# First batch's first half: pair 2's division moved behind row copies, pair 3's product moved to VectorE, the first gate groups issued a step sooner

## The chip, the cores and the metric

The kernel runs on one core of one Trainium2 chip. The metric is the device time of one execution in microseconds. The core's engines work side by side and wait for one another through semaphores: TensorE (PE in the profile; its weight loads are PEld), VectorE (DVE), ScalarE (ACT), GpSimd (POOL) and SyncE (SP), which here only issues DMAs. Each engine takes its instructions in the order in which the program lists them for it.

## The reference

Inputs are `q`, `k`, `v` of shape (4, 8, 768, 64) (batch, head, token, width), 16 centroids per head, and three weight matrices. The first stage is attention inside clusters, the second a gated feed-forward layer on its output:

```python
q_assign = np.argmax(np.einsum('bhsd,hcd->bhsc', q_n, c_n), axis=-1)
k_assign = np.argmax(np.einsum('bhsd,hcd->bhsc', k_n, c_n), axis=-1)
mask = q_assign[:, :, :, None] == k_assign[:, :, None, :]
scores = scale * np.matmul(q, k.transpose(0, 1, 3, 2))
scores = np.where(mask, scores, -1000000000.0)
...
attn = attn / (np.sum(attn, axis=-1, keepdims=True) + 1e-09)
return np.matmul(attn, v).astype(np.float32)
...
gate = 1.0 / (1.0 + np.exp(-(x @ w_gate)))
val = x @ w_val
return (gate * val @ w_out).astype(np.float32)
```

`x` holds the 3072 tokens by 512 (8 heads of 64); `w_gate` and `w_val` are 512 x 1536, `w_out` is 1536 x 512.

## The kernel before

Heads are worked in four pairs per batch. For each head the kernel splits `q` and `k` into a high and a low 16-bit part (`hl`), turns them so that the width lies across partitions (`T`), multiplies with the centroids (`lg`, logits), takes the largest (`mx`) and writes a one-hot row per token (`oh`). The one-hots are turned too (`oh_ps`) and copied into rows 64 to 79 of `T`: these are the **row copies** (L1396 for the keys, L1400 for the queries of a part, on DVE or, at L1398, on ACT). So one matmul `sc` (L1066) gives score and mask at once. ACT takes the exponential `es` (L1071), and three short matmuls `av` (L1089) multiply it with the values, to which a column is added that sums the weights.

A **step** is one such piece: 128 keys of a head against 384 queries, one `sc`, one `es`, three `av`. There are 384 steps. The `av` of a step stand a few steps behind its `sc` (three in the first batch, `la0`). The first batch is cut into two halves of its queries: all eight heads on the first 384 tokens (steps 0 to 47), then all eight on the others.

When both heads of a pair are through, `normalise2` (first batch; later batches use `normalise`) ends them: DVE adds a correction `sv` to the sums `av` and writes `t` (L384), DVE takes the reciprocal `rec` of the weight column (L389), POOL multiplies and writes `xp` (L390). In the first half, and for pair 0 of the second, `turn_x` then turns `xp` on PE (`x_ps`, L1117) and DVE copies the result into `xTb` (L1118), which the feed-forward layer reads.

The feed-forward work is a queue of pieces: for each of 12 column blocks a gate group (four matmuls `g`, L532, and a tanh `th` on ACT, L538), a value group (four matmuls `v`, L548, and a product `hT` on DVE, L553), then output groups (`o`). `ffn_block` puts a half's pieces into the queue at a step that the table sets: the end of its steps plus a lag, `lag00` for the first batch's first half. From then on `ffn_run` takes pieces from the queue at each step, as many as a budget of nanoseconds per step allows (`ns02` is 490).

All other work stands in a table by step too: `SCHED` maps names to steps, counted from the step at which a pair is first used, and `at(step, f)` runs `f` when the loop comes to that step. The order in which the loop writes instructions is the order of each engine. `xt30` and `xm30` set the step of the turn of pair 3's `xp`. `b1p2l20` chooses how the logits of batch 1, pair 2, head 0 are made: not zero takes `logits2`, two matmuls of 16 columns for each of 12 blocks, summed in PSUM (L423); zero takes `logits`, one matmul of 32 columns per block (L436), whose two halves a reduction on DVE then adds (`lgs`, L451). `b1p2lg0` and `b1p2pk0`, -35.5 steps from use, set when this happens. Hops of later heads (DMAs of one-hot rows into `T`) are issued 12 steps or more ahead of use.

Four PSUM banks (`bank`) go round among `sc`, `g`, `v`, `lg` and `x_ps`.

Of the kernel before, what the change touches and what calls it, by code (L numbers as in the profile page):

```python
# [11 lines left out]
ALU = mybir.AluOpType  # L12
# [83 lines left out]
    "fwv": [354, 356, 357, 359, 364, 366, 370, 371], "b3p2pk1": -28.5, "END": 0,  # L96
}


# [1 line left out]
def kernel(  # L101
# [12 lines left out]
    PE, ACT, DVE, POOL, SP = nc.tensor, nc.scalar, nc.vector, nc.gpsimd, nc.sync  # L114
# [250 lines left out]
    def bcast(ap, n):  # L365
        return ap.unsqueeze(len(ap.shape)).to_broadcast(list(ap.shape) + [n])

    def normalise(av, nq, b, p, e, x, eng=None):

        t = tmpp.tile([128, NCH, 65], FP, name="t")  # L370
        sv = SV[b, p][:, e, :].unsqueeze(1).to_broadcast([128, nq, 65])
        DVE.tensor_tensor(t[:, 0:nq, :], av, sv, ALU.add)  # L372
        rec = smp.tile([128, NCH], FP, name="rec")
        DVE.reciprocal(  # L374
            rec[:, 0:nq], t[:, 0:nq, 64:65].rearrange("p c x -> p (c x)")
        )
        (eng or POOL).tensor_tensor(x, t[:, 0:nq, 0:64], bcast(rec[:, 0:nq], 64), ALU.mult)  # L377

    def normalise2(av, nq, b, p, x):
        t = tmpp.tile([128, NCH, 65], FP, name="t")
        sv = SV[b, p].unsqueeze(2).to_broadcast([128, 2, nq, 65])
        DVE.tensor_tensor(  # L384
            t.rearrange("p (e c) d -> p e c d", e=2), av.rearrange("p (e c) d -> p e c d", e=2),
            sv, ALU.add,
        )
        rec = smp.tile([128, NCH], FP, name="rec")
        DVE.reciprocal(rec, t[:, :, 64:65].rearrange("p c x -> p (c x)"))  # L389
        POOL.tensor_tensor(  # L390
            x.rearrange("p c (e d) -> p e c d", e=2),
            t[:, :, 0:64].rearrange("p (e c) d -> p e c d", e=2),
            bcast(rec.rearrange("p (e c) -> p e c", e=2), 64), ALU.mult,
        )

    T = {}

# [676 lines left out]
    def do_av(s):  # L1074
        b, p, e, nq = s["b"], s["p"], s["e"], s["nq"]
        first, last = s.get("first", False), s.get("last", False)
        need(("v", b, p, e))
        both = nq == 3 and b < SCHED.get("pn", 0)
        if first:
            if not both:  # L1080
                cur["av"] = avp.tile([128, nq, 65], FP, tag="av", name="av")
            elif e == 0:
                cur["av"] = avp.tile([128, 2 * nq, 65], FP, tag="av", name="av")
            if e == 0:
                cur["x"] = xpp.tile([128, nq, 128], HP, tag="xp", name="xp")
        av, x = cur["av"], cur["x"]
        a0 = nq * e if both else 0
        for i in range(s["n"]):
            PE.matmul(  # L1089
                out=av[:, a0 + s["c0"] + i, :], lhsT=s["es"][:, bass.ts(i, 128)],  # L1090
                rhs=VA[b, p][:, e, s["j"], :],
                start=(first and i == 0 and a0 == 0),
                stop=(last and i == s["n"] - 1 and (e == 1 or not both)), skip_group_check=True,
            )
        if last:
            if not both:
                normalise(av, nq, b, p, e, x[:, :, bass.ts(e, 64)])
            elif e == 1:
                normalise2(av, nq, b, p, x)
            if e == 1:  # L1100
                f = lambda: turn_x(b, p, x, 128 * s["h0"], nq, s["xT"])
                if b == 0 and SCHED.get(f"xm{p}{3 * s['h1']}", p == 3):
                    at(step_no[0] + SCHED.get(f"xt{p}{3 * s['h1']}", 5), f)
                else:
                    d_ = SCHED.get(f"xs{min(b, 1)}{p}", 0)
                    if d_ > 0 and (b < B - 1 or p < 2):
                        at(step_no[0] + d_, f)
                    else:
                        f()

    def turn_x(b, p, x, o, nq, xT):
        done.update(("x", b, p, o // 128 + c) for c in range(nq))
        dst = xT[:, p, o : o + 128 * nq].rearrange("p (c t) -> p c t", t=128)
        if b == 0 and SCHED.get(f"xm{p}{3 * [z for z, _ in PARTS].index(o // 128)}", p == 3):
            ps = (turns if SCHED.get("lgop", 1) else bank)(NCH * 128, HP, name="x_ps")
            for c in range(nq):
                PE.transpose(ps[:, bass.ts(c, 128)], x[:, c, :], identh)  # L1117
            DVE.tensor_copy(xT[:, p, o : o + 128 * nq], ps[:, 0 : 128 * nq])  # L1118
        else:
            SP.dma_start_transpose(out=dst, in_=x.rearrange("p c t -> p (c t)"))  # L1120

    bg = {}
    step_no = [-4]

    def at(i, f):
        bg.setdefault(max(i, step_no[0] - 0.5), []).append(f)
# [11 lines left out]
    def need(*names):  # L1138
        for n in names:
            assert n in done, n  # L1140
# [441 lines left out]
    for b, p, e in P:  # L1582
        if b + p + e == 0:
            continue
        d = P[b, p, e]
        for k_, o_ in (OFF if b else FIRST).items():
            f = d.get(k_[:2])
# [114 lines left out]
    for b in range(B):  # L1702
# [17 lines left out]
        for p, e, c in heads(b):  # L1720
            for s in head_steps(b, p, e, c):
                s["xT"] = xT
                do_scores(s)
                run_bg(step_no[0] - 0.5)
                pend.append(s)
                r = step_no[0] - BASE[b]
                ns = SCHED.get(f"ns{b}{r // 24}", SCHED.get(f"ns{b}", 500.0))
                ns += SCHED.get(f"nx{step_no[0]}", 0)
                ffn_run(ns if b or r >= DONE0[0] else 0.0)
                while len(pend) > LA[min(b, 1)]:  # L1730
                    do_av(pend.pop(0))
                run_bg(step_no[0])
                step_no[0] += 1
    while pend:
        ffn_run(500.0)
        do_av(pend.pop(0))
# [34 lines left out]
```

## Time and profile before

| | us |
|---|---|
| median of 3 runs | 319.01 |
| lowest and highest | 318.76, 319.01 |
| the profiled execution | 319.12 |
| its span | 317.3 |
| PE busy in the span | 310.0 |
| ACT busy | 244.9 |
| DVE busy | 238.6 |
| POOL busy | 120.9 |

The span runs from the first to the last instruction, and times in rows of the trace count from its start; 1.8 us of the execution lie around it. A row of the timeline gives start, duration, engine, line, operation, output and inputs, shapes and count, and in brackets how long the engine was idle before and what ended that. Matmuls are pipelined: a matmul of 384 columns shows 0.33 us, while the next can start 0.16 us after it.

### The profile page before, as it was taken

Reading aid. Unit: us, or ns where it says so; the run is one execution under the profiler, and the core shown is the slowest. Engines: PE = TensorE matmul, PEld = TensorE weight load, DVE = VectorE, ACT = ScalarE, POOL = GpSimd, SP = SyncE. Lnnn points to the kernel's source line nnn. Section 1 sums busy time; section 2 is a strip of 40 time slices with the busy share of each in tenths; the row PEclk is TensorE's granted clock in tenths of the full one; section 3 lists DMA queues with packets and bytes.
Section 4 is the critical chain, followed back from the end, with each engine's and each line's share of the span. In section 5 each row is a group of like instructions: output and inputs, shape, how many; then the busy total and the mean of one; then the engine's idle time right before and its main releaser. Section 6 shows DMA issues by size and latency. Waiting matters only on the chain.

```text
span 317.3 us, 9228 instructions
## 1 busy us (share of the span) xinstructions
PE 310.0 (98%) x3492; PEld 218.8 (69%) x3492; DVE 238.6 (75%) x623; ACT 244.9 (77%) x555; POOL 120.9 (38%) x157
## 2 busy tenths in 40 slices
PE   7899999999999999999999999999999999999995
PEld 4688766766666666666777678766677678656685
DVE  5899756778688777686788688776888776678983
ACT  6688998797899887877776876777877887588621
POOL 5888454244434275423234333424212111026600
PEclk9999999999999999999999999999999999999999
DMA  7999998639848988976676455882506130300014
GB/s 196 379 259 169 271 164 143 176 83 264 242 100 163 204 221 136 199 217 161 106 193 153 151 118 134 248 153 53 112 2 76 55 27 14 145 1 3 0 35 165
DMA packets 77996, 45.16 MB, mean 142 GB/s; under 512 B 56896, under 2 KB 75520, under 8 KB 77952
## 3 DMA queue, kind: packets, MB, share of 16 engines
q1 hardware_dynamic: 73840, 39.66, 51.3%
q0 software_dynamic: 3680, 4.72, 9.1%
q8 instruction: 27, 0.44, 0.6%
q10 hardware_dynamic: 432, 0.20, 0.2%
q14 instruction: 17, 0.14, 0.1%
HBM read 28.34 MB, written 6.29 MB: 109 GB/s over the span
## 4 chain that ended last, share of the span: by engine, by line
PE 93%; DMA 2%; DVE 1%; POOL 1%; SPq 1%; issue 0%; ACT 0%; DVEq 0%
PE sc L1066 19%; PE g L532 15%; PE v L548 15%; PE av L1089 11%; PE o L994 9%; PE o L865 5%; PE lg L436 2%; PE o L699 2%; PE o_end L802 2%; PE av L699 2%; DMA kraw<-in_k_dram 2%; PE v L628 2%; PE y L699 2%; PE o L802 1%; PE av L802 1%; PE z L699 1%
## 5 line engine op out<-in xcount | busy, mean ns | idle before, releaser
L1071 ACT ACTIVATE es<-sc 128x384 f16<-128x384 f32 x384 | 174.1, 492 | 38.5 <-PE sc L1066 29.8
L1066 PE MATMUL sc<-T 128*128 128x384 f16 x384 | 117.3, 325 | 0.7 <-DVE T L1396 0.4
L1089 PEld LDWEIGHTS <-es 128*128 128x128 f16 x1152 | 81.3, 98 | 35.1 <-ACT es L1071 0.2
L1089 PE MATMUL av<-va,es 128*128 128x65 f16 x1152 | 97.6, 194 | 0.0
L553 DVE SCALAR_TENSOR_TENSOR hT<-th,v 128x384 f16<-128x384 f32 x72 | 39.8, 553 | 33.8 <-PE av L1089 29.6
L377 POOL TENSOR_TENSOR xp<-t,rec 128x384 f16<-128x384 f32 (+1 forms) x30 | 21.8, 726 | 97.3 <-DVE rec L374 49.2
L548 PE MATMUL v<-xTb,wv 128*128 128x384 f16 x288 | 58.5, 326 | 0.1
L532 PE MATMUL g<-xTb,wg 128*128 128x384 f16 x288 | 58.5, 326 | 0.0
L538 ACT ACTIVATE th<-g 128x384 f32<-128x384 f32 x72 | 35.4, 492 | 8.3 <-PE g L532 6.3
L1066 PEld LDWEIGHTS <-T 128*128 128x128 f16 x384 | 37.0, 96 | 1.2 <-DVE T L1396 0.7
L548 PEld LDWEIGHTS <-wv 128*128 128x128 f16 x288 | 28.0, 97 | 13.9 <-issue 0.3
L532 PEld LDWEIGHTS <-wg 128*128 128x128 f16 x288 | 27.9, 97 | 13.9
L1632 POOL TENSOR_TENSOR hl<-kraw,hl 128x384 f16<-128x384 f32 x22 | 20.2, 920 | 40.6 <-DVE hl L1631 25.9
L1632 POOL TENSOR_TENSOR hl<-qraw,hl 128x384 f16<-128x384 f32 x22 | 21.1, 961 | 11.1 <-DVE hl L1631 11.1
L865 PE MATMUL o<-wo,hT 128*128 128x512 f16 x72 | 19.9, 379 | 0.0
L372 DVE TENSOR_TENSOR t<-av,sv 128x390 f32<-128x390 f32 (+1 forms) x30 | 14.4, 480 | 7.1 <-PE av L1089 5.3
L941 DVE TENSOR_TENSOR ob<-o,ob 128x256 f32<-128x256 f32 (+1 forms) x28 | 15.0, 549 | 4.7 <-PE o L994 3.2
L708 POOL TENSOR_TENSOR hT<-T 128x384 f16<-128x384 f32 x12 | 11.8, 1001 | 16.2 <-DVE T L657 15.6
L994 PE MATMUL o<-wo,hT 128*128 128x256 f16 x108 | 16.8, 272 | 0.0
L994 PEld LDWEIGHTS <-sum 128*128 128x128 f16 x144 | 14.0, 97 | 3.3
L451 DVE TENSOR_REDUCE lgs<-lg 128x192 f32<-128x384 f32 x23 | 12.7, 551 | 3.0 <-PE lg L436 2.9
L324 POOL CAST va<-vraw 128x768 f16<-128x768 f32 x15 | 13.1, 873 | 2.4 <-DMA vraw<-in_v_dram 2.4
(225 smaller groups left out, 470.2 us busy)
## 6 DMA issues: line engine op xcount, KB each, us to landing
vraw<-in_v_dram SPq DMA_DIRECT2D x15, 384.0 KB, 4.9
kraw<-in_k_dram SPq DMA_DIRECT2D x14, 384.0 KB, 4.2
qraw<-in_q_dram SPq DMA_DIRECT2D x12, 384.0 KB, 4.1
out_dram<-ob SPq DMA_DIRECT2D x17, 256.0 KB, 2.2
wg<-in_moe_w_gate_dram POOLq DMA_DIRECT2D x2, 768.0 KB, 9.2
wv<-in_moe_w_val_dram POOLq DMA_DIRECT2D x2, 768.0 KB, 10.4
wo<-in_moe_w_out_dram POOLq DMA_DIRECT2D x2, 768.0 KB, 9.3
T<-ohT SPq DMA_DIRECT2D x44, 24.0 KB, 1.9
```

What stands on the lines that cost most here:

```text
L377: (eng or POOL).tensor_tensor(x, t[:, 0:nq, 0:64], bcast(rec[:, 0:nq], 64), ALU.mult)
L532: PE.matmul(out=g[:, 0:n], lhsT=wg[fc // WQ][:, dc, fc % WQ, :], rhs=xT[:, dc, t0 : t0 + n], start=(dc == 0), stop=(dc == NDC - 1),)
L538: ACT.activation(th[:, 0:n], g[:, 0:n], AF.Tanh)
L548: PE.matmul(out=w[:, 0:n], lhsT=wv[fc // WQ][:, dc, fc % WQ, :], rhs=xT[:, dc, t0 : t0 + n], start=(dc == 0), stop=(dc == NDC - 1),)
L553: DVE.scalar_tensor_tensor(HB[b, blk][:, fc, 0:n], st[0][:, 0:n], 1.0, w[:, 0:n], ALU.add, ALU.mult)
L699: PE.matmul(out=o, lhsT=l, rhs=r, start=start and d == 0, stop=stop and d == 1, skip_group_check=True,)
L865: PE.matmul(out=o, lhsT=HB[b, blk][:, fc, bass.ts(t, 128)], rhs=wo[fc // WON][:, fc % WON, :], start=(fc == 0), stop=(fc == NFC - 1),)
L994: PE.matmul(out=st[z][:, e], lhsT=a[:, c, :], rhs=rhs[:, c, :], start=start and c + e == 0, stop=c == HF - 1, skip_group_check=True,)
L1066: PE.matmul(out=sc.rearrange("p (c t) -> p c t", t=128), lhsT=s["k"], rhs=s["q"], start=True, stop=True,)
L1071: ACT.activation(es, sc, AF.Exp, scale=SCALE)
L1089: PE.matmul(out=av[:, a0 + s["c0"] + i, :], lhsT=s["es"][:, bass.ts(i, 128)], rhs=VA[b, p][:, e, s["j"], :], start=(first and i == 0 and a ...
L1632: POOL.tensor_tensor(hl[:, :, 64:128], r, hl[:, :, 0:64], ALU.subtract)
```

## The change

`normalise2` is told at which query half it works (`h0`). Its reciprocal and product become a function `divide`. It runs at once, as before, unless the table has an entry `nW<pair><h0>`: then it is put off by so many steps. An entry `nE<pair><h0>` puts the product on DVE instead of POOL. Two entries are added, for pair 2 (`nW20`: 2.2 steps later) and pair 3 (`nE30`: product on DVE) of the first half; `lag00` goes from 8 to 7, so the first half's feed-forward pieces enter the queue a step sooner; and `b1p2l20` goes from 1.5 to 0, so that one head's logits in batch 1 take the other form.

```diff
-    "b1p2vs": -11.0, "b1p2vu": -2.5, "b1p2vt": 3, "b1p2ld": -67.5, "b1p2l20": 1.5, "b1p2le0":
+    "b1p2vs": -11.0, "b1p2vu": -2.5, "b1p2vt": 3, "b1p2ld": -67.5, "b1p2l20": 0, "b1p2le0":
...
-    4.0, "lag00": 8, "lag01": 4.5, "lag10": 7.5, "lag11": 5.5, "ns0": 460, "ns1": 410, "ns10":
+    4.0, "lag00": 7, "lag01": 4.5, "lag10": 7.5, "lag11": 5.5, "ns0": 460, "ns1": 410, "ns10":
...
-    "fwv": [354, 356, 357, 359, 364, 366, 370, 371], "b3p2pk1": -28.5, "END": 0,
+    "fwv": [354, 356, 357, 359, 364, 366, 370, 371], "b3p2pk1": -28.5, "nW20": 2.2, "nE30": 1, "END": 0,
...
-    def normalise2(av, nq, b, p, x):
+    def normalise2(av, nq, b, p, x, h0):
...
-        DVE.reciprocal(rec, t[:, :, 64:65].rearrange("p c x -> p (c x)"))
-        POOL.tensor_tensor(
-            x.rearrange("p c (e d) -> p e c d", e=2),
-            t[:, :, 0:64].rearrange("p (e c) d -> p e c d", e=2),
-            bcast(rec.rearrange("p (e c) -> p e c", e=2), 64), ALU.mult,
-        )
+
+        def divide():
+            DVE.reciprocal(rec, t[:, :, 64:65].rearrange("p c x -> p (c x)"))
+            (DVE if SCHED.get(f"nE{p}{h0}", 0) else POOL).tensor_tensor(
+                x.rearrange("p c (e d) -> p e c d", e=2),
+                t[:, :, 0:64].rearrange("p (e c) d -> p e c d", e=2),
+                bcast(rec.rearrange("p (e c) -> p e c", e=2), 64), ALU.mult,
+            )
+
+        w = SCHED.get(f"nW{p}{h0}", 0)
+        at(step_no[0] + w, divide) if w else divide()
...
-                normalise2(av, nq, b, p, x)
+                normalise2(av, nq, b, p, x, s["h0"])
```

The function grows by five lines, so lines behind it have numbers higher by five in the changed kernel (the row copy L1396 becomes L1401, the score L1066 becomes L1071).

DVE at the turn from pair 2 to pair 3 of the first half, before; `oh_ps` is the turned one-hot of the last pair's heads, `T` their turned keys and queries:

```order
L384 TENSOR_TENSOR t<-av,sv 128x390
L389 RECIPROCAL rec<-t 128x6
L1400 TENSOR_SCALAR T<-oh_ps 16x384
L1396 COPY T<-oh_ps 16x768
L1451 TENSOR_REDUCE mx<-lg_1037 128x6
L1452 TENSOR_TENSOR oh_136<-lg_1037,mx 128x2x3x16
```

The same place now:

```order
L384 TENSOR_TENSOR t<-av,sv 128x390
L1405 TENSOR_SCALAR T<-oh_ps 16x384
L1401 COPY T<-oh_ps 16x768
L391 RECIPROCAL rec<-t 128x6
L1456 TENSOR_REDUCE mx<-lg_1035 128x6
L1457 TENSOR_TENSOR oh_136<-lg_1035,mx 128x2x3x16
```

The reciprocal has moved behind the two row copies.

DVE at the end of pair 3 and the start of the second half, before; `hT` are the feed-forward products, the second `t` and `rec` are those of pair 0 in the second half:

```order
L384 TENSOR_TENSOR t<-av,sv 128x390
L389 RECIPROCAL rec<-t 128x6
L1451 TENSOR_REDUCE mx<-lg_1167 128x6
L1452 TENSOR_TENSOR oh_134<-lg_1167,mx 128x2x3x16
L1400 TENSOR_SCALAR T<-oh_ps 16x384
L1118 COPY xTb<-x_ps 128x384
L553 SCALAR_TENSOR_TENSOR hT<-th,v 128x384 x2
L1631 CAST hl<-kraw 128x6x64
L384 TENSOR_TENSOR t<-av,sv 128x390
L389 RECIPROCAL rec<-t 128x6
L553 SCALAR_TENSOR_TENSOR hT<-th,v 128x384
```

The same place now:

```order
L384 TENSOR_TENSOR t<-av,sv 128x390
L391 RECIPROCAL rec<-t 128x6
L392 TENSOR_TENSOR xp<-t,rec 128x2x3x64
L1456 TENSOR_REDUCE mx<-lg_1167 128x6
L1457 TENSOR_TENSOR oh_134<-lg_1167,mx 128x2x3x16
L1405 TENSOR_SCALAR T<-oh_ps 16x384
L1123 COPY xTb<-x_ps 128x384
L558 SCALAR_TENSOR_TENSOR hT<-th,v 128x384 x2
L1636 CAST hl<-kraw 128x6x64
L558 SCALAR_TENSOR_TENSOR hT<-th,v 128x384
L384 TENSOR_TENSOR t<-av,sv 128x390
L391 RECIPROCAL rec<-t 128x6
```

The product `xp` is new between the reciprocal and the next head's `mx` and `oh`, and the third `hT` has moved ahead of pair 0's `t`.

ACT where the first gates come in, before; 20 exponentials stand between a copy of turned queries and the first tanh:

```order
L1071 ACTIVATE es<-sc 128x384 x20
L538 ACTIVATE th<-g 128x384
L1398 ACTIVATE T<-oh_ps 16x384
L1071 ACTIVATE es<-sc 128x384 x2
L538 ACTIVATE th<-g 128x384
```

The same place now:

```order
L1076 ACTIVATE es<-sc 128x384 x19
L543 ACTIVATE th<-g 128x384
L1076 ACTIVATE es<-sc 128x384
L1403 ACTIVATE T<-oh_ps 16x384
L1076 ACTIVATE es<-sc 128x384
L543 ACTIVATE th<-g 128x384
```

The first tanh has moved ahead of one exponential, and every later feed-forward piece likewise by about a step. On PE the turn of the one-hot `oh_134` (`oh_ps`) stands ahead of the turn of pair 3's `xp` (`x_ps`) in both.

## The prediction

> **What bounds the kernel now.** I read the page's chain first, then busy times by stretch, then the stretch that the change touches, engine by engine. The chain by engine, and the stretches (length; PE, PEld, DVE, ACT and POOL busy; clock, DMA share, GB/s):
>
> ```profile
> PE 93%; DMA 2%; DVE 1%; POOL 1%; SPq 1%; issue 0%; ACT 0%; DVEq 0%
> 32.00:40.00 8.00, 7.51 (x124) 5.61 (x122) 5.54 (x17) 7.74 (x20) 3.51 (x5) 1.00 1.07 266
> 40.00:80.00 40.00, 40.00 (x445) 26.44 (x444) 28.30 (x72) 33.64 (x77) 17.03 (x21) 1.00 0.76 164
> 80.00:160.00 80.00, 80.00 (x917) 53.39 (x916) 58.89 (x159) 67.81 (x157) 32.27 (x37) 1.00 0.80 174
> ```
>
> PE is never idle from 40 to 160 us, at the full granted clock. So from 40 us on the end moves by only two things: when PE becomes full, and how much work it then has. The change sits where PE is not yet full, 32 to 40 us. First place there, the turn from pair 2 to pair 3:
>
> ```profile
> 31.79 0.56 DVE L384 TENSOR_TENSOR t<-av,sv 128x390 f32<-128x390 f32 x1
> 32.39 0.19 DVE L389 RECIPROCAL rec<-t 128x6 f32<-128x6 f32 x1
> 32.61 0.36 DVE L1400 TENSOR_SCALAR T<-oh_ps 16x384 f16<-16x384 f16 x1
> 32.98 0.56 DVE L1396 COPY T<-oh_ps 16x768 f16<-16x768 f16 x1
> 31.82 0.49 PE L1375 MATMUL oh_ps<-identh,oh 128*128 128x128 f16 x6
> 33.60 0.34 PE L1066 MATMUL sc<-T 128*128 128x384 f16 x1 [0.38 <-DVE T L1396]
> 32.66 0.82 POOL L390 TENSOR_TENSOR xp<-t,rec 128x384 f16<-128x384 f32 x1 [1.46 <-DVE rec L389]
> 34.70 0.33 PE L1117 MATMUL x_ps<-identh,xp 128*128 128x128 f16 x3
> 32.23 6.91 ACT L1071 ACTIVATE es<-sc 128x384 f16<-128x384 f32 x17
> ```
>
> The last head's first scores wait 0.38 us for its row copies. These stand behind the reciprocal of pair 2, though their input, the turned one-hot, has left PE at 32.31. ACT runs its 17 exponentials almost without a gap beside it. Second place, the end of pair 3:
>
> ```profile
> 36.89 0.56 DVE L384 TENSOR_TENSOR t<-av,sv 128x390 f32<-128x390 f32 x1 [0.36 <-PE av L1089]
> 37.49 0.19 DVE L389 RECIPROCAL rec<-t 128x6 f32<-128x6 f32 x1
> 37.59 0.22 DVE L1451 TENSOR_REDUCE mx<-lg 128x6 f32<-128x96 f32 x1
> 37.85 0.26 DVE L1452 TENSOR_TENSOR oh<-lg,mx 128x96 f16<-128x96 f32 x1
> 38.57 0.36 DVE L1400 TENSOR_SCALAR T<-oh_ps 16x384 f16<-16x384 f16 x1 [0.46 <-PE oh_ps L1470]
> 39.02 0.36 DVE L1118 COPY xTb<-x_ps 128x384 f16<-128x384 f16 x1
> 37.76 0.82 POOL L390 TENSOR_TENSOR xp<-t,rec 128x384 f16<-128x384 f32 x1 [3.83 <-DVE rec L389]
> 38.20 0.33 PE L1470 MATMUL oh_ps<-identh,oh 128*128 128x128 f16 x3
> 38.64 0.11 PEld L1117 LDWEIGHTS <-xp 128*128 128x128 f16 x2 [0.28 <-POOL xp L390]
> 39.58 0.33 PE L532 MATMUL g<-xTb,wg 128*128 128x384 f16 x1
> ```
>
> PE turns the one-hot `oh` at 38.20, as soon as DVE has it (38.11), then waits 0.28 us for POOL's product `xp`. From 38.64 on it is back to back into the first gate matmul at 39.58.
>
> **The change part by part.**
>
> *Reciprocal behind the row copies.* The copies can start when `t` ends, 0.03 us later as the reciprocal did (32.39 instead of 32.61), so the scores come 0.22 us earlier. The reciprocal then starts near 33.36, and behind it pair 2's product on POOL near 33.63 instead of 32.66; it ends at 34.45 and its turn on PE is wanted at 34.70 − 0.22 = 34.48: weights have to be loaded first, so I take 0.03 back. `oh` of that place keeps its time, because the reciprocal only changes sides with the copies. **−0.19 us**. Bounds: 0, if ACT's row of exponentials holds PE anyway, and −0.22. I take nearly all of it, since ACT's 6.91 us contain one restart just after this wait and PE is the engine that is waited for there.
>
> *Last pair's product on DVE.* No run shows this product on DVE. The nearest row is a group of two-input operations on 384 float32 values per partition (shortest, median and longest in ns):
>
> ```profile
> L332 DVE TENSOR_TENSOR va<-vraw x12: 523/551/1175, 69.5 to 241.4; 128x384 f32<-128x384 f32 x12
> ```
>
> I take 0.55 us; the ends are 0.35 (the one-input copy of 384 values at 39.02 above, 0.36) and 1.18 (the longest of the twelve). It saves the 0.82 us on POOL, but `mx` and `oh` now stand behind it on DVE, and on PE the turn of `oh` stands ahead of the turn of `xp`. Worked in the old times: product 37.71 to 38.26, `mx` starts 0.08 before that ends (as it did behind the reciprocal) and ends at 38.40, `oh` 38.44 to 38.70, its turn on PE at 38.79 (0.09 behind, as now), and three turns of 0.055 later the turn of `xp` at 38.96 instead of 38.64: **+0.32 us**. The wait for POOL goes, and a longer one for `oh` takes its place. With the ends of the product it is +0.12 to +0.95. What is queued behind: the copy `T` and the copy `xTb`, which follow PE's turns by 0.37 and 0.36 as before.
>
> The Trainium skill would price this lower. Its page GPSIMD Engine Reference, section 3.1 Elementwise, has a large addition 1.96 times slower on GpSimd than on VectorE; from the POOL row's 0.82 that gives an estimate of 0.42 us on DVE and a sum lower by 0.13. I hold to the rows of this size.
>
> *First gates a step sooner.* PE's list gets the first gate group behind the second, not the third, score after `xp`'s turn. PE is back to back from that turn on, so order alone gives **0**. What hides it: only the group's fourth matmul reads the last pair; it comes three times 0.16 us after the first. Counted from `oh`'s turn, the copies end at about +1.12 (0.37 + 0.36, 0.36, 0.03), the fourth matmul stands at 0.17 + 0.17 + 4 groups of scores and averages (0.51) + 0.49 = +1.34. Without that cover of 0.2 us each 0.1 of lateness costs 0.1. All gates, values and stores of the later batches move about a step against the rest, on SP too (three stores stand one transpose or hop earlier); the heads' hops are due a dozen steps later, so I cost SP at nothing, and at a late hop's full delay if that lead is gone.
>
> One place moves to the worse: in the second half, the third hidden product stands ahead of pair 0's `t`.
>
> ```profile
> 44.80 0.57 DVE L384 TENSOR_TENSOR t<-av,sv 128x390 f32<-128x390 f32 x1 [0.42 <-PE av L1089]
> 45.61 0.55 DVE L553 SCALAR_TENSOR_TENSOR hT<-th,v 128x384 f16<-128x384 f32 x1
> 45.67 0.82 POOL L390 TENSOR_TENSOR xp<-t,rec 128x384 f16<-128x384 f32 x1 [0.30 <-DVE rec L389]
> 46.90 0.28 PE L1117 MATMUL x_ps<-identh,xp 128*128 128x128 f16 x2
> ```
>
> `xp` ends at 46.49 and is turned at 46.90: 0.41 us of room, 0.47 us taken (0.55 less the overlap). With the weight load, **+0.1 us**, from 0 to 0.3. Other flips of this kind in 280 us I take as nought: after 40 us the chain leaves PE only once before the end, for a tanh on ACT:
>
> ```profile
> 183.38 0.50 ACT th L538
> ```
>
>
> *POOL and the two DMAs of `wo`.* These rows stand behind pair 3's product now, and come about 3 us sooner without it, as do the issues of `wo` between and behind them. `wo` is read first at 66 us:
>
> ```profile
> 38.54 0.91 POOL L1415 TENSOR_TENSOR hl<-qraw,hl 128x384 f16<-128x384 f32 x1
> 40.28 0.52 POOL L1411 CAST hl<-qheld 128x384 f16<-128x384 f32 x1
> 66.38 0.88 PE o L865 x4
> ```
>
> Cost 0: nothing waits for them so early.
>
> *Logits in batch 1, pair 2, head 0.*
>
> ```profile
> 80.95 0.75 PE L423 MATMUL lg<-cm,T 128*128 128x16 f16 x24
> 81.55 0.32 PE L532 MATMUL g<-xTb,wg 128*128 128x384 f16 x1
> 93.96 0.45 PE L436 MATMUL lg<-cm,T 128*128 128x32 f16 x12
> 94.26 0.32 PE L1066 MATMUL sc<-T 128*128 128x384 f16 x1
> 94.45 0.56 DVE L451 TENSOR_REDUCE lgs<-lg 128x192 f32<-128x384 f32 x1
> 81.74 0.36 DVE L462 TENSOR_REDUCE mx<-lg 128x12 f32<-128x192 f32 x1 [1.67 <-PE lg L423]
> ```
>
> 24 matmuls hold PE for 0.60 us (80.95 to 81.55), 12 of the wide kind for 0.30 (93.96 to 94.26). PE is full there: **−0.30 us**. DVE gets one reduction of 0.56 us, covered by the 1.67 us that it idled; without that cover, 0.56 on its next product.
>
> **Sum:** −0.19 + 0.32 + 0 + 0.1 − 0.30 = **−0.07 us**. The profiled execution took 319.12 us, which gives 319.05; the median of the runs shown, 319.01, lies 0.11 lower, so the forecast for a median is **318.9 us**: no change that can be told. About 0.2% (0.64 us) is what a measurement of this kernel can tell from no change.
>
> **Rivals.**
>
> *The wait really goes (faster).* If the turn of pair 3 does not have to wait for `oh`, all three gains count: −0.22 − 0.28 − 0.30 = −0.80, **318.2**. For it: each wait stands in a row above, and with a product of 0.35 us the second is nearly met. Against it: `oh` is behind the product on DVE and ahead on PE.
>
> *The product meets POOL (slower).* The mechanism is in this trace:
>
> ```profile
> 46.90 0.69 DVE L1452 TENSOR_TENSOR oh<-lgs,mx 128x96 f16<-128x96 f32 x1
> 46.45 1.03 POOL L1415 TENSOR_TENSOR hl<-qheld,hl 128x384 f16<-128x384 f32 x1
> ```
>
> The same one-hot that takes 0.26 us from PSUM at 37.85 takes 0.69 here, both operands in SBUF, until POOL's split ends. The product's operands both lie in SBUF. If a POOL operation is running when it starts (37.5 us in the new times), it waits for that one's end: up to 1.18 − 0.55 = 0.63 by the longest row, which makes the sum +0.56, **319.5**; with the 0.91 us of a whole split, 319.8. Against it: counted on from pair 2's product, which ends at 34.45 (a cast of 0.5, a split of 0.9, a DMA issue of 0.9), POOL's cast of the held query runs from about 36.7 to 37.2, with a DMA issue after it; it decides from about 0.3 us of lateness on POOL. The Trainium skill's page SBUF — State Buffer, section Who interferes with whom, states it as a rule: a VectorE instruction with two SBUF inputs contends with a GpSimd one that reads SBUF, and who starts first holds the port. By that rule, the trace agrees with 0.69 against 0.26 us.
>
> *The move does nothing.* If ACT holds PE from 33 to 36 us and the reciprocal's move gives 0, the sum is +0.12: **319.1**, inside the forecast.
>
> **How the numbers follow.** Forecast, with the last rival inside it (318.4 to 319.4): 0.55. Faster: 0.24. Slower, by POOL or by new waits of the moved products: 0.21. The low end of the range is the first rival, 318.2; the high end, 319.7, is short of the second's worst. Faster by over 0.2% (under 318.37): 0.24; within: 0.54; slower (over 319.65): 0.22, its half of the POOL rival and an unforeseen wait of 0.7 us or more in the 280 us that are written in another order.
>
> **What would show it.** In the changed profile: no or a short wait of the scores for `T`, 33.4 us instead of 33.6; a wait of about 0.6 us of PE's weight load for `oh` near 38 us, none for `xp`; the product on DVE at 0.55 us, POOL's share down by 0.8 us; 24 matmuls fewer by 12, one `lgs` reduction more; PE full from 40 us on. I am wrong if the product takes 0.4 or 0.9 us, if PE idles after 40 us, or if SP's moved stores make a head wait.

## The result, and the profile after

The changed kernel takes **322.04 us** (median of 4 runs, 321.01 to 322.43) against 319.01 for the kernel before beside it: ratio 1.0091, 95% interval 1.0067 to 1.0116. It is 3 us slower; the forecast was 318.9, with a range up to 319.7. The profiled execution took 321.96 us, its span is 320.1 (before 317.3).

The page's chain by engine, of the changed kernel:

```profile
PE 92%; DVE 4%; ACT 1%; DMA 1%; issue 0%; ACTq 0%; DVEq 0%
```

DVE had 1% of this chain; now it has 4%. The stretches of the changed kernel (length; PE, PEld, DVE, ACT and POOL busy; clock, DMA share, GB/s):

```profile
40.00:80.00 40.00, 38.94 (x431) 25.71 (x429) 27.52 (x67) 32.19 (x73) 15.23 (x18) 1.00 0.68 151
80.00:160.00 80.00, 79.58 (x898) 52.28 (x895) 61.11 (x161) 67.33 (x155) 31.82 (x38) 1.00 0.76 177
```

The clock is full as before. PE was busy for 40.00 and 80.00 us in these two; now it idles 1.06 and 0.42 us. The time goes where the change's own rows do not stand. First the place where they do, on DVE and on PE:

```profile
37.45 0.56 DVE L392 TENSOR_TENSOR xp<-t,rec 128x384 f16<-128x384 f32 x1
...
38.21 0.26 DVE L1457 TENSOR_TENSOR oh<-lg,mx 128x96 f16<-128x96 f32 x1
```

```profile
33.27 0.34 PE L1071 MATMUL sc<-T 128*128 128x384 f16 x1 [0.15 <-DVE T L1401]
...
37.77 0.32 PE L1071 MATMUL sc<-T 128*128 128x384 f16 x1
38.53 0.34 PE L1475 MATMUL oh_ps<-identh,oh 128*128 128x128 f16 x3 [0.43 <-DVE oh L1457]
...
39.38 0.81 PE L537 MATMUL g<-xTb,wg 128*128 128x384 f16 x4
```

The scores wait 0.15 us for `T` in place of 0.38. The product takes 0.56 us on DVE; PE waits 0.43 us for `oh` (0.59 counted by the starts of its matmuls; about 0.6 was forecast) and no longer for `xp`. The first gates start at 39.38, 0.16 us behind the scores of 39.22, so back to back. All of this is as forecast, within 0.1 us. Then come waits that the kernel before does not have. PE's waits from 36 us to the end, grouped (total, times, longest); the view leaves out short ones:

```profile
PE oh_ps L1255 <- DVE oh L1234: 0.7, 1, 0.7
PE oh_ps L1475 <- DVE oh L1457: 0.4, 1, 0.4
PE sc L1071 <- DVE hT L558: 0.4, 1, 0.4
PE g L537 <- DVE hT L558: 0.2, 1, 0.2
```

The first and the third are the largest. The third, on all engines around 48 us of the changed kernel:

```profile
46.83 0.81 PE L553 MATMUL v<-xTb,wv 128*128 128x384 f16 x4
...
47.12 0.68 DVE L1636 CAST hl<-qraw 128x384 f16<-128x384 f32 x1
47.54 1.03 POOL L1420 TENSOR_TENSOR hl<-qheld,hl 128x384 f16<-128x384 f32 x1
...
47.72 0.24 DVE L1456 TENSOR_REDUCE mx<-lgs 128x6 f32<-128x96 f32 x1
47.73 0.33 PE L1122 MATMUL x_ps<-identh,xp 128*128 128x128 f16 x3
...
47.99 0.69 DVE L1457 TENSOR_TENSOR oh<-lgs,mx 128x96 f16<-128x96 f32 x1
...
48.61 0.54 DVE L558 SCALAR_TENSOR_TENSOR hT<-th,v 128x384 f16<-128x384 f32 x1
...
49.20 0.32 PE L1071 MATMUL sc<-T 128*128 128x384 f16 x1 [0.40 <-DVE hT L558]
```

The value group `v` ends on PE at 47.64. Its product `hT` could start about then, but the pick `mx`, `oh` now stands ahead of it on DVE, and `oh` takes 0.69 us while POOL splits `hl`. `hT` ends at 49.15, and PE's next scores wait for it: it reads the bank of PSUM that they take over (value group, scores, turn of `xp` and gates have taken the four). In the kernel before the value group stood a step later and its product behind this pick, which took 0.69 us there too (46.90 to 47.59):

```profile
47.13 0.81 PE L548 MATMUL v<-xTb,wv 128*128 128x384 f16 x4
...
48.05 0.55 DVE L553 SCALAR_TENSOR_TENSOR hT<-th,v 128x384 f16<-128x384 f32 x1 [0.18 <-PE av L1089]
```

DVE was idle for 0.18 us ahead of that product, and no matmul waited for it. The other wait, on DVE and on PE:

```profile
75.39 0.69 DVE L878 COPY ob<-o 128x512 f32<-128x512 f32 x1 [1.84 <-PE o L870]
76.00 0.34 DVE L1231 TENSOR_REDUCE mx<-lgs 128x12 f32<-128x192 f32 x1
76.38 0.43 DVE L1234 TENSOR_TENSOR oh<-lgs,mx 128x96 f16<-128x96 f32 x2
```

```profile
75.89 0.32 PE L1071 MATMUL sc<-T 128*128 128x384 f16 x1
76.86 0.51 PE L1255 MATMUL oh_ps<-identh,oh 128*128 128x128 f16 x6 [0.66 <-DVE oh L1234]
```

And the same rows of the kernel before:

```profile
71.80 0.34 DVE L1226 TENSOR_REDUCE mx<-lgs 128x12 f32<-128x192 f32 x1
72.18 1.04 DVE L1229 TENSOR_TENSOR oh<-lgs,mx 128x96 f16<-128x96 f32 x2
75.18 0.69 DVE L873 COPY ob<-o 128x512 f32<-128x512 f32 x1
75.23 0.50 PE L1250 MATMUL oh_ps<-identh,oh 128*128 128x128 f16 x6
```

Before, the pick was done 2 us ahead of its turn on PE. Now the output copy `ob`, a piece of the feed-forward work, has moved ahead of it on DVE; the copy waits 1.84 us for its matmuls, and the pick, whose input has long been there, waits behind it. The Trainium skill's page Perfetto Trace Analysis, section Tensor Engine Instruction (MATMUL, LD_WEIGHTS), calls VectorE's queue strictly first in, first out; these rows agree.

The idle time understates the loss. A matmul of 384 columns shows 0.32 us, but inside a group the next one starts 0.16 us later (the group of four above takes 0.81 = 3 × 0.16 + 0.33). So a gap of up to 0.16 us leaves no idle time at all. Counted by the starts of PE's matmuls, the wait at 49 us is 0.57, that at 76 us 0.82, and there are fourteen more from 46 to 278 us, of 0.07 to 0.37 each: 3.6 us in all, where the kernel before has 0.4. (One of the fourteen, 0.29 at 130.78, is a wait for a DMA.) With the other three edits as the traces below size them, +0.33 for the product, -0.16 for the reciprocal and -0.30 for the matmuls saved, this makes an estimate of 3.6 - 0.4 + 0.33 - 0.16 - 0.30 = +3.1 us. The medians gave +3.0.

### The profile page after: what moved, and what is told of

Its sections match the earlier page's. It is cut to its first block, busy times and chain, and to the rows that moved or that the text cites. A ratio compares the mean times of both kernels' runs of the same rounds, so it can differ in the third digit from the quotient of the medians.

```text
span 320.1 us, 9200 instructions
## 1 busy us (share of the span) xinstructions
PE 312.4 (98%) x3480; PEld 220.5 (69%) x3480; DVE 240.6 (75%) x625; ACT 244.5 (76%) x555; POOL 120.0 (37%) x156
## 4 chain that ended last, share of the span: by engine, by line
PE 92%; DVE 4%; ACT 1%; DMA 1%; issue 0%; ACTq 0%; DVEq 0%
PE sc L1071 18%; PE v L553 15%; PE g L537 14%; PE av L1094 10%; PE o L999 9%; PE o L870 5%; PE lg L441 2%; PE o L704 2%; PE o_end L807 2%; PE av L704 2%; PE y L704 2%; PE v L633 2%; PE av L807 1%; PE o L807 1%; PE t_ps L1320 1%; PE lg L428 1%
## 5 line engine op out<-in xcount | busy, mean ns | idle before, releaser
L1071 PE MATMUL sc<-T 128*128 128x384 f16 x384 | 117.3, 326 | 0.6 <-DVE hT L558 0.4
L1071 PEld LDWEIGHTS <-T 128*128 128x128 f16 x384 | 37.1, 97 | 0.4 <-DVE T L1401 0.3
```

The source lines that it names most:

```text
L1071: PE.matmul(out=sc.rearrange("p (c t) -> p c t", t=128), lhsT=s["k"], rhs=s["q"], start=True, stop=True,)
```

## The experiments

The theory: the loss comes from the first gates a step sooner alone. The table's background work has fixed steps; the feed-forward queue, once started a step sooner, stays a step sooner for the rest of the kernel, and each place where a feed-forward row changes sides with a background row can make a wait. The rival: one of the other three edits makes the waits. The ratio in the table is not that of the two medians beside it: for e3 the medians give +0.37 us, the ratio +0.7.

| run | what differs from the kernel before | median us | before beside it | ratio, 95% interval |
|---|---|---|---|---|
| the change | all four edits | 322.04 | 319.01 | 1.0091 (1.0067 to 1.0116) |
| e1 | three edits, gates at their old step | 318.94 | 319.12 | 0.9990 (0.9976 to 1.0005) |
| e2 | gates a step sooner | 321.55 | 319.12 | 1.0079 (1.0062 to 1.0097) |
| e3 | product on VectorE | 319.49 | 319.12 | 1.0022 (1.0008 to 1.0037) |
| e4 | reciprocal behind the row copies | 318.81 | 319.27 | 0.9985 (0.9967 to 1.0003) |
| e5 | logits in 12 wide matmuls | 318.91 | 319.27 | 0.9996 (0.9980 to 1.0011) |
| e6 | reciprocal and logits | 318.52 | 319.12 | 0.9972 (0.9959 to 0.9985) |
| e12 | the same as e6 | 318.71 | 319.14 | 0.9983 (0.9971 to 0.9996) |
| e7 | e2, two picks moved | 320.56 | 319.13 | 1.0052 (1.0029 to 1.0076) |
| e8 | e2, old order again from step 80 | 320.25 | 319.13 | 1.0040 (1.0022 to 1.0058) |
| e10 | new order only from step 80 | 321.28 | 319.13 | 1.0071 (1.0047 to 1.0095) |
| e11 | e2, old order again from step 60 | 320.18 | 319.27 | 1.0026 (1.0004 to 1.0047) |
| e9 | gates a step later | 323.59 | 319.13 | 1.0130 (1.0109 to 1.0150) |

### Which edit: e1 and e2

e1 is the changed kernel with one edit undone, e2 the kernel before with that edit alone:

```
e1   -    "lag00": 7
     +    "lag00": 8
e2   -    "lag00": 8
     +    "lag00": 7
```

> The changed kernel with the first gates put back to their old step; the reciprocal, the product on VectorE and the logits of batch 1 stay changed. Theory (the loss is in the order of the later work, which the earlier gates write anew): the loss goes, and what is left is -0.19 + 0.32 - 0.30 of the prediction, 318.8 to 319.0 us, ratio 0.999 to 1.001. Rival (the product on VectorE, the reciprocal or the logits make the new waits): it stays near the changed kernel, 321.5 to 322.4, ratio 1.008 to 1.011.

> The kernel before with one edit, the first gates a step sooner. Theory (order of the later work): nearly the whole loss, +2.5 to +3.3 us, 321.5 to 322.3, ratio 1.008 to 1.010. Rival (the loss needs the moved product or the other edits): 318.8 to 319.4, ratio 0.999 to 1.001.

The theory's numbers came out in both: 318.94 and 321.55. With the gates at their old step no wait of PE behind 40 us is left in this view; PE's waits of e1 and of e2 from 36 us on:

```profile
PE oh_ps L1475 <- DVE oh L1457: 0.4, 1, 0.4
```

```profile
PE oh_ps L1255 <- DVE oh L1234: 0.7, 1, 0.7
PE sc L1071 <- DVE hT L558: 0.4, 1, 0.4
...
```

e2 has the changed kernel's waits, with the same lengths, and not the one of the moved product. The rival is out: the loss needs none of the other edits.

### The other parts alone: e3, e4, e5

```
e3   +    "nE30": 1
e4   +    "nW20": 2.2
e5   -    "b1p2l20": 1.5
     +    "b1p2l20": 0
```

> The kernel before with one edit, the last pair's product of the first half on VectorE. The prediction's term: +0.32 us (0.12 to 0.95), 319.3, ratio 1.001, with a wait of PE's weight load for oh of about 0.6 us near 38 us in place of the 0.28 us for xp. Rival (this edit is the cause of the loss): 321 to 322.

e3, PE and DVE around the product:

```profile
38.70 0.56 DVE L392 TENSOR_TENSOR xp<-t,rec 128x384 f16<-128x384 f32 x1
...
39.02 0.32 PE L1071 MATMUL sc<-T 128*128 128x384 f16 x1
...
39.77 0.34 PE L1475 MATMUL oh_ps<-identh,oh 128*128 128x128 f16 x3 [0.43 <-DVE oh L1457]
...
39.95 0.33 PE L1122 MATMUL x_ps<-identh,xp 128*128 128x128 f16 x3
```

From the start of the scores ahead of it (39.02) to the turn of `xp` (39.95) it is 0.93 us; in the kernel before those scores start at 38.04 and the turn at 38.64, 0.60 us. The price is 0.33 us, and the first gates behind it lose 0.08 more (below). The runs agree: +0.37 us by the medians, 0.3 to 1.2 by the interval (0.08% to 0.37%). The product takes 0.56 us here, in e1 and in the changed kernel.

> The kernel before with one edit, the reciprocal of pair 2 behind the row copies of the last head. The prediction's term: -0.19 us (0 to -0.22), 318.9, ratio 0.9994, and the scores' wait of 0.38 us for T near 33 us shrinks to about 0.15. Rival (ACT's row of exponentials holds PE there anyway): the wait moves on, 319.1, ratio 1.000.

e4, the last row copy on DVE and the scores behind it:

```profile
32.64 0.56 DVE L1401 COPY T<-oh_ps 16x768 f16<-16x768 f16 x1
...
33.25 0.34 PE L1071 MATMUL sc<-T 128*128 128x384 f16 x1 [0.15 <-DVE T L1401]
```

The wait shrinks from 0.38 to 0.15 us, and the scores come 0.22 us sooner. Two steps later 0.06 of that is lost again (0.32 us from scores to scores in place of 0.26). So the four steps around the wait take 1.71 us in every kernel with this edit and 1.87 in those without: 0.16 us. The runs, -0.46 us with an interval that holds zero, can't tell so little.

> The kernel before with one edit, the logits of batch 1, pair 2, head 0 at their new place, where they are formed with 12 wide matmuls in place of 24. The prediction's term: -0.30 us, 318.8, ratio 0.999, PE full before and behind it. Rival (the reduction of 0.56 us that VectorE gets makes something wait): 319.1 to 319.5, ratio 1.000 to 1.001.

e5, PE at the new logits:

```profile
80.74 0.45 PE L441 MATMUL lg<-cm,T 128*128 128x32 f16 x12
81.21 0.65 PE L537 MATMUL g<-xTb,wg 128*128 128x384 f16 x3
```

Twelve matmuls at 0.025 us apiece end at 81.04, but the gate starts only at 81.21: 0.17 us of the 0.30 saved turn into a wait, which ends as ACT's next exponential does (in e6 the exponential of 79.88 ends at 80.36 and the gate starts at 80.41). The trace has 0.13 us of gain behind this place; the runs, -0.36 us with an interval that holds zero, can't tell it. What the gate waits for is read from these times and was not tried by itself.

### Where in the kernel: e8, e10, e11

The budget of a step can be changed by an entry `nx<step>`. Taking one step's 490 ns away at step 80 (near 60 us) brings the feed-forward queue back to the old steps from there on; adding them at step 80 to the kernel before starts the new order there.

```
e8   +    "lag00": 7, "nx80": -490
e10  +    "nx80": 490
e11  +    "lag00": 7, "nx60": -490
```

> The kernel before with the first gates a step sooner, and one step's share of feed-forward work left out at step 80 (60 us), so that from there on each list stands as before. Theory: only the waits up to there are left, 0.08 + 0.57 us, 319.1 + 0.65 = 319.8 us, ratio 1.002. Rival (the loss is set by the start of the gates, whatever comes later): 321.5, ratio 1.008.

> The kernel before with its first gates at their old step, and one step's share of feed-forward work added at step 80 (60 us): the order is that of before up to there, and that of the step-sooner run from there on. Theory: the waits from 60 us on alone, +1.9 us (2.5 less 0.65), 321.0 us, ratio 1.006. Rival (the start of the gates makes the loss): 319.1, ratio 1.000.

Both halves lose, by +1.12 and +2.15 us (e2: +2.43), so neither the start of the gates nor any one place makes the loss. e10 came out near the expected 321.0, at 321.28. e8 cost 0.5 more than the theory's waits. Its trace has the known ones at 46 and 48 us (0.08 and 0.57), 0.12 us at 62 and a new one at 78: the scores at 77.80 are followed by the `av` only at 78.26, 0.46 us in place of 0.16, as they wait for an exponential on ACT, which stands behind a copy of 0.80 us. That is 1.07 in all. The lists of PE, DVE, ACT and POOL are those of the kernel before from 60 us on; why ACT is later there is open. The profiled execution of e8 also has a late DMA (below), which its median does not show.

> The kernel before with the first gates a step sooner, and one step's share of feed-forward work left out at step 60, three steps behind: only the first gates stand sooner, VectorE's list is that of before from end to end. Theory (the first gates themselves cost nothing, the later order does): no wait that before does not have, 319.1 us, ratio 0.999 to 1.001. Rival (the first gates meet the last pair of the first half): a wait of their fourth matmul near 39 us and 319.4 or more.

This missed. The list of DVE is that of the kernel before, row by row; those of PE and ACT differ between 39 and 44 us only; and yet it lost 0.9 us by the medians (interval 0.04% to 0.47%). The first gates themselves do not wait, so the rival's mechanism isn't there either. What happens stands later, from 45 us on:

```profile
47.00 0.92 POOL L1420 TENSOR_TENSOR hl<-qheld,hl 128x384 f16<-128x384 f32 x1
47.11 1.02 DVE L1636 CAST hl<-qraw 128x384 f16<-128x384 f32 x1
...
48.21 0.91 POOL L1637 TENSOR_TENSOR hl<-qraw,hl 128x384 f16<-128x384 f32 x1 [0.29 <-DVE hl L1636]
48.33 0.91 DVE L1457 TENSOR_TENSOR oh<-lgs,mx 128x96 f16<-128x96 f32 x1
...
49.16 0.34 DVE L1123 COPY xTb<-x_ps 128x384 f16<-128x384 f16 x1
...
49.56 0.65 PE L537 MATMUL g<-xTb,wg 128*128 128x384 f16 x3 [0.40 <-DVE xTb L1123]
```

The empty step lets three scores follow each other without gates between, ACT falls behind with its exponentials, the next value group starts 0.3 us late, and with it DVE's rows. They then run into POOL's splits: the cast takes 1.02 us and the one-hot 0.91, where the kernel before has 0.46 (its row at 46.25) and 0.69. Counted by the starts, PE loses 0.32 us at that value group, 0.10 at the gates behind it and 0.56 at the gates of 49.56: 0.97 in all. So the same order on each engine from 44 us on can still cost time when a few rows start some tenths later against POOL's. My theory spoke of order alone; these rows say order and phase. No run changed the phase by itself.

### Two collisions mended: e7

```
e7   +    "lag00": 7
     -    "r2pk": 64.0      "g1pk": 96.0
     +    "r2pk": 65.0      "g1pk": 95.5
```

> The kernel before with the first gates a step sooner, and two picks of one-hots moved by a step so that they change sides with one feed-forward row on VectorE each: the one at 48 us behind the product hT, the one at 75 us ahead of the copy ob. Theory (the loss is a row of single collisions in VectorE's list): the two largest waits of the step-sooner run go, 0.57 and 0.82 us, so 321.55 - 1.39 = 320.2 us, ratio 1.0035; the other waits behind them stay. Rival (the earlier gates make the kernel slower as a whole, and a wait that is mended shows up elsewhere): 321.2 to 321.8, ratio 1.0065 to 1.0085.

On DVE this swaps two pairs of rows against e2 and nothing else: `hT` ahead of the pick at 48 us, the pick ahead of `ob` at 75 us. e7 around these places:

```profile
47.23 1.03 POOL L1420 TENSOR_TENSOR hl<-qheld,hl 128x384 f16<-128x384 f32 x1
...
47.41 0.54 DVE L558 SCALAR_TENSOR_TENSOR hT<-th,v 128x384 f16<-128x384 f32 x1
...
48.15 0.26 DVE L1457 TENSOR_TENSOR oh<-lgs,mx 128x96 f16<-128x96 f32 x1
...
72.98 1.04 DVE L1234 TENSOR_TENSOR oh<-lgs,mx 128x96 f16<-128x96 f32 x2
74.52 0.69 DVE L878 COPY ob<-o 128x512 f32<-128x512 f32 x1 [0.49 <-PE o L870]
```

```profile
75.01 0.32 PE L1071 MATMUL sc<-T 128*128 128x384 f16 x1
75.17 0.50 PE L1255 MATMUL oh_ps<-identh,oh 128*128 128x128 f16 x6
```

Both waits are gone: the turn of the one-hot starts 0.16 us behind the scores, as in an unbroken row. The span falls from 320.0 (e2) to 318.7, 1.3 us; counted from the turn of pair 3's `xp` (38.22 and 38.38) to the end, it is 1.5. The medians fall by 0.99, from 321.55 to 320.56; the intervals of the two ratios overlap, so here the traces carry the argument. The two waits are thus the cause of four tenths of e2's loss by the medians, half by the spans, and they do not come up elsewhere. The smaller ones from 80 to 220 us stay; each was only seen, not tried.

### A step to the other side: e9

```
e9   -    "lag00": 8
     +    "lag00": 9
```

> The kernel before with the first gates a step later, at 9 steps behind the first half in place of 8 (the change has 7). Theory (the background work is fitted to one order, and a shift to either side collides with it): slower as well, +1 to +3 us, ratio 1.003 to 1.010. Rival (only earlier gates cost, since they take the reserve between a product and its use): 318.9 to 319.6, ratio 0.9995 to 1.0015.

It is slower still, +4.5 us. Its largest wait:

```profile
77.22 0.68 DVE L878 COPY ob<-o 128x512 f32<-128x512 f32 x1
...
77.95 0.81 PE L870 MATMUL o<-wo,hT 128*128 128x512 f16 x3 [0.93 <-DVE ob L878]
```

The same copy is now late itself, and PE's next outputs wait for its bank. In the kernel before it stood ahead of two rows of DVE, `va` and `vs`; here it stands behind them, and they take 0.92 and 0.90 us. So sooner isn't bad in itself: of seven, eight and nine steps, eight is the fastest. That the table's other steps were fitted to eight would explain it; it is not shown.

### What is left as a gain: e6 and e12

Both have the reciprocal and the logits of the change and nothing else; e12 is a second measurement.

> The changed kernel without the two edits that the prediction priced at a loss or nothing: the reciprocal behind the row copies and the logits of batch 1 are kept, the product is on GpSimd again and the first gates stand at their old step. By the prediction's terms -0.19 - 0.30 = -0.49 us, 318.5, ratio 0.9985. Rival (any edit that moves work in time makes new waits): over 319.6, ratio over 1.002.

> The kernel with the reciprocal and the logits alone once more, since its first runs gave -0.60 us (ratio 0.9972) where its own trace accounts for about -0.3 us behind 32 us (-0.16 at the scores' wait, -0.13 behind the logits). If the trace tells all: 318.8 us, ratio 0.999. If the runs do: 318.5, ratio 0.997.

-0.60 and -0.43 us, both intervals below 1. This is the fastest of the kernels here, 0.2% to 0.3% under the kernel before. The traces account for 0.16 + 0.13 = 0.29 us of it. e12's interval holds that (0.1 to 0.9 us), e6's does not (0.5 to 1.3); whether there is more to gain than the traces show is open.

## Why the prediction was wrong, point by point

**The step that failed** is "First gates a step sooner", and in it the sentence "Other flips of this kind in 280 us I take as nought". The term was 0 + 0.1 us; e2 measured it at +2.43 (2.0 to 3.1). The reason given was that the chain leaves PE only once after 40 us. That describes one order. It says that nothing waits there now, not how much room each row has, and 280 us of rows were about to change sides. The sign named for it came: PE idles for 1.06 us from 40 to 80 us. Even the single flip that I did price came out otherwise. I had the turn of pair 0's `xp` late by 0.1 us, but it starts at 47.73, 0.16 us behind its scores, so nothing waits: the value group of 46.83 has moved ahead of it on PE and covers its lateness. What PE loses there, 0.08 us at 46.83, comes as a tanh on ACT ends (46.78), and the kernel before has 0.07 of the kind at 47.13. That 0.1 and 0.08 are near each other is chance. What was missing is a look at each engine's whole list, PE's too. The pick at 72 us had 2 us of room, and a row that moved ahead of it took them and 0.8 more.

**The local claim held.** The first gates themselves wait for nothing (39.38, back to back), in the changed kernel and in e11.

**Reciprocal:** -0.19 forecast, -0.16 in the traces. The rival that ACT holds PE there would have left nothing, and fell. What takes 0.06 of the 0.22 away two steps later is open.

**Product:** +0.32 forecast, +0.33 measured. In e1 and e3 the first gates also start 0.08 us later behind their scores (39.27 to 39.51 in e1); in the changed kernel they don't. I took 0.55 us for it by the nearest rows; it takes 0.56. The estimate of 0.42 by the Trainium skill's page GPSIMD Engine Reference, section 3.1 Elementwise, was too low for this size: 0.82 on POOL is 1.47 times the 0.56 on DVE, not 1.96.

**Logits:** -0.30 forecast, -0.13 in the traces. The 12 matmuls do save 0.30 us, but the gate behind them then waits 0.17. "PE is full there" left out that the next matmul could be limited by its bank.

**POOL and `wo`:** 0, as forecast. The issues of `wo` come at 35.7 and 37.1 us in place of 39.4 and 40.7, and nothing waits for them.

**SP's moved stores:** nothing was forecast, with a late hop as the sign of being wrong. In the changed kernel's profiled execution no head's logits or scores wait for a DMA behind 36 us; PE waits once for a transposed `xTb` (130.78). Other runs have late transposes (last section), some with SP's list unchanged, so whether the moved stores add to the medians stays open.

**The rivals.** "The wait really goes" fell, since PE waits 0.43 us for `oh`, as the forecast had it. "The product meets POOL" fell for this product, which takes 0.56 us in every kernel that has it; but its mechanism, a DVE row that lengthens beside POOL's split, is part of the wait at 48 us. "An unforeseen wait of 0.7 us or more in the 280 us" is what came. It stood as a remnant within 0.22 for slower, with the price of one wait, though the text had already said that every later piece moves.

## What to carry to other kernels

Where one table fixes the steps of some work and a queue feeds the rest, a shift of the queue's start is not a local edit: list, for the whole length, which rows change sides on each engine that works in order, and take the room that each has from the trace (here 2 us of room at one pick did not help, since the row that moved ahead of it waits 1.84 us itself). A bounding engine that never idles says that all waits are covered in this order, not that they are covered with room to spare. Split an edit of several parts before judging it: two of the four together gain 0.3 us by the traces (0.4 and 0.6 by the runs), one loses 0.4 and one loses 2.4.

## What the runs showed of the hardware that was not expected

**A one-hot on DVE takes 0.26 to 0.91 us, by its phase to POOL.** It has two operands in SBUF, as has POOL's split. In e7 it starts at 48.15, 0.11 us ahead of the end of POOL's split (47.23 + 1.03 = 48.26): 0.26. In the changed kernel it starts at 47.99 into a split that ends at 48.57, and ends at 48.68: 0.69. In e11 it starts 0.12 us behind the start of a split that ends at 49.12, and ends at 49.24: 0.91. In the last two it ends 0.11 to 0.12 us behind the end of POOL's row, whenever it started; in e9 too (0.45 us, to 47.58, with a split that ends at 47.46). By the rule of the Trainium skill's page SBUF — State Buffer, section Who interferes with whom, such an instruction waits for the GpSimd one that holds the port; these rows agree. The cast of `qraw`, with one operand, lengthens too: 0.46 us before, 0.68 in the changed kernel, 1.02 in e11 and 1.09 in e9. In all four it ends 0.21 to 0.22 us behind the end of the POOL row beside it; the cast of `kraw` at 73.21 of the changed kernel, with POOL idle, takes 0.35.

**A transposing DMA lands later in some executions.** PE of e8:

```profile
123.16 0.46 PE L441 MATMUL lg<-cm,T 128*128 128x32 f16 x12 [1.38 <-DMA T<-hl]
```

The transpose that these logits wait for, issued at 115.9 us, lands 7.2 us after its issue. The same transpose takes 4.2 us in the kernel before, 5.1 in e3, 5.7 in e4 and 5.6 in e11. In e3, e4, e8 and e11 the DMA issues on SP stand in the order of the kernel before from end to end, and the other engines' lists are those of before for the 50 us ahead of it. PE's waits for such transposes are 1.38 us in e8, 0.82 in e10, 0.27 in e4, 0.23 in e11, 0.12 in e7 and 0.11 in e2; the profiled executions of the kernel before and of e1, e3, e5, e6 and e12 have none. Each kernel was profiled once, so that one kernel differs from execution to execution is not shown directly. That e8's profiled execution took 321.64 us and its median is 320.25, 1.39 less, agrees with it.
